# A new work order, an earlier Exp table and ten idle products in a state-space plus gated-MLP kernel

## The chip, the cores and the metric

The kernel runs on one core of a Trainium2 chip. The time is that of one execution on the device, in microseconds (us). The core has five engines that run side by side, each with its own queue of instructions: TensorE (PE in the profile; PEld is its weight load), VectorE (DVE), ScalarE (ACT), GpSimd (POOL) and SyncE (SP), which here only issues DMA transfers. An engine takes its instructions strictly in the order in which the program lists them: one that waits holds up all behind it.

## The reference: what is computed

The input `u` is 2048 tokens of 512 channels. It is normalised, and two branches work on the result; their sum and `u` are the output.

```python
xn = _layernorm(x, axis=-1)
# A: a long convolution along the tokens, its kernel built from 128 complex modes a channel
P = jnp.exp(logdA[:, :, None] * l[None, None, :])
K = jnp.einsum("dn,dnl,dn->dl", Cc, P, dB).real
y = irfft(rfft(xn) * rfft(K)) [:L] + xn * Dskip
# B: a gated MLP with 1792 hidden channels
h = sigmoid(xn @ w_gate) * (xn @ w_up);  out_B = h @ w_down
return x + y + out_B
```

(The two middle lines are shortened.) Inputs and output are bf16.

## The kernel before, in words

**What the work is.** The tokens are 16 tiles of 128. `layernorm` takes their statistics: for tiles 0 to 3 with `bn_stats` on DVE (`stat`, L443 and L445) or, for tiles 1 and 3, in another way on ACT (`stat_act`, L449 to L451). `rstd0` (L457 to L470) makes the reciprocal deviations of tiles 0 to 3 on DVE. `rstd` does it for tiles 4 to 7 on POOL, and for tiles 8 to 15 on POOL too (L479 to L510). Then each tile is normalised (`norm` on DVE, L514, or `norm2` on ACT, L519) and transposed: groups 0 and 1 on TensorE (L524), groups 2 and 3 by DMA (L547).

`params` turns the mode parameters into powers: the time step is `exp(log_dt)` on ACT (L596), a diagonal of it is made on DVE (`dg`, L597, needs the identity), and TensorE multiplies the raw parameters by it (L608, L613). ACT takes four exponentials (L621) and one plain eviction (L624); DVE makes phases (L632 to L637), ACT sines (L640, L641, L646), and DVE and ACT products of them (L654 to L730). An ACT function of another table needs a table load; two tiny activations (L594) make ACT load the Exp and the Sin table at a chosen place.

`glu` is branch B in four groups of 512 tokens: products with gate and up weights (L781), sigmoid on ACT (L807), product on DVE (L814 or L819), down projection (L785), evictions, and adding DMA writes to the output issued by POOL (L840).

Branch A goes by eight chunks of 64 channels: `tables` builds powers of the modes on DVE with squares on ACT (L1244 to L1246, L888 to L892); `kgen`, or for the last two chunks `kgen_late`, multiplies them on TensorE (L976) and transforms them (L946, L999, L1005). `spectrum_x1` and `spectrum_x2` transform the tokens (L762, L1078), `freq` multiplies the spectra (L1125, L1145, L1133 or L1136), and `outq` transforms back and writes (L1192, L1206, L1209, L1212, L1227).

**How it is ordered.** Each step is registered with `add(...)`: engine, an estimate of its time, the steps it comes after, a rank, and sometimes `alt`, a second engine that can do it. Two lists at the end of the file go by the numbers that the steps get in this way. `TURN` is the order in which the steps are written into the program, for all engines; each engine's queue is the part of it that is its own. `OTHER` names the steps that run on their `alt` engine. The estimates are for the planner that made the lists; the program itself only reads `TURN` and `OTHER`:

```python
    def order(self):
        for t in (self.tasks[n] for n in OTHER):
            t.eng, t.cost, t.fn = t.alt[:3]
        return [self.tasks[n] for n in TURN]
```

So everything that the change does to the program lies in the two lists and in the two steps that it adds. In the head, steps 0 to 21 are loads: 0 and 1 the first token tiles, 2 the identity, 3 `s1`, 4 `log_dt`, 5 to 10 the raw parameters (8 is the imaginary part of C), 13, 17 and 16 the token groups 1, 3 and 2, the others MLP weights. Step 101 sets two constants on POOL, 102 to 104 are the seed, the Exp table and `exp(log_dt)`, 105 the diagonal, 26 to 29 the statistics of tiles 0 to 3, 30 is `rstd0`, 43 and 60 are the two `rstd` on POOL, 52 to 59 the statistics of tiles 8 to 15, and 61, 62, 71, 72, 81, 82, 91, 92 their norms.

PSUM tiles come from two pools: `ps_m` with four banks, and `ps_gu` with two pairs of banks (tag `gu`), which the MLP's `pg` and `pu`, and late in the kernel `pw` and `ptv`, take in turn.

Of the kernel before, what the change touches and what calls it, by code (L numbers as in the profile page):

```python
# [11 lines left out]
F32 = mybir.dt.float32  # L12
I32 = mybir.dt.int32
ACT = mybir.ActivationFunctionType
# [237 lines left out]
class _Kernel:  # L252
    def __init__(self, ctx, tc, ins, out):
# [22 lines left out]
        for k in range(len(BLOCKS)):  # L276
            self.freq(k)
            self.outq(k)
        with tc.manual_schedule(engines=ENGINES):
            self.p.emit()  # L280
# [152 lines left out]
    def layernorm(self):  # L433
        nc, add, c = self.nc, self.p.add, self.mult
# [92 lines left out]
        for lo, hi in ((0, 1), (1, 2), (2, 4)):  # L527
            st = [add("DVE", 0.69 if lo else 0.87, lambda i=i: stat(i), [self.ld[f"x{i // 4}{i // 2 * 2 if i < 4 else 0}"]],
                      R["LN2"] + i if lo else R["LN"], use=[self.xg[i // 4]], alt=("ACT", 1.5, lambda i=i: stat_act(i), R["LN"]) if i in (1, 3) else None)
                  for i in range(4 * lo, 4 * hi)]  # L530
            slow = lambda lo=lo, hi=hi: rstd(lo, hi, nc.gpsimd)
            r = add("POOL", 20.0, slow, st, R["LN2"] + 10 * lo) if lo == 1 else add(
                "DVE", 4.2 if lo else 3.4, (lambda lo=lo, hi=hi: rstd(lo, hi, nc.vector)) if lo else rstd0, st, R["LN2"] + 10 * lo if lo else R["LN"],
                alt=("POOL", 16.0, slow, R["LN2"] + 10 * lo) if lo else None)
            self.rstd.append(r)
            for i in range(4 * lo, 4 * hi, 2):
# [5 lines left out]
                if g > 1:  # L542
                    self.norm += n
                    for k in range(2):
                        for kt in range(KT):
# [10 lines left out]
                                          use=[pt, xnT[g]]))  # L556
# [675 lines left out]
def _level(nc, l, o, m, tB, rs, step):  # L1232
# [124 lines left out]
```

## Time and profile before

| | |
|---|---|
| time, median of 3 runs (lowest, highest) | 268.34 us (267.07, 268.83) |
| the profiled execution's own time | 268.08 us |
| its span, first to last instruction | 266.3 us |
| mean granted TensorE clock | 0.990 |
| busy: PE, DVE, ACT, POOL | 236.8, 240.3, 227.8, 65.7 us |
| share of the span | 89%, 90%, 86%, 25% |
| chain that ended last, by engine | PE 44%, DVE 21%, ACT 20%, POOL 6%, issue 5% |
| HBM traffic | 24.61 MB read, 15.73 MB written |

The times are device times of whole executions; the profile is of one of them. Busy time counts an engine's instructions and not the waits of its queue. Matmuls are pipelined and their ends are modelled, so a fully busy PE isn't PE at its peak. A timeline row gives start, duration, engine, line, operation, what it writes and reads, and in brackets how long the engine was idle before it and what ended that. `ACTq` and `SPq` rows are the issue of a DMA by that engine's queue.

### The profile page before, as it was taken

The numbers are of one execution on the slowest core, as the hardware profiler recorded it, in microseconds if no ns is written. First come the engines' busy times: TensorE is split into PE (matmuls) and PEld (weight loads), VectorE is DVE, ScalarE is ACT, GpSimd is POOL, SyncE is SP. The second block draws the span as 40 slices with busy tenths as digits, with TensorE's granted clock in tenths as the row PEclk, the third lists the DMA queues.
The fourth block names the chain that finished last, engine by engine and source line by source line (L and its number), as shares of the span: only waits on it lengthen the run. The fifth ranks groups of instructions, "written<-read, shape, count | busy, mean of one in ns | idle before, by whom it ended". The sixth has DMA issues, their size and how long they took to land.

```text
span 266.3 us, 5528 instructions
## 1 busy us (share of the span) xinstructions
PE 236.8 (89%) x2040; PEld 137.4 (52%) x2040; DVE 240.3 (90%) x450; ACT 227.8 (86%) x369; POOL 65.7 (25%) x107
## 2 busy tenths in 40 slices
PE   0556899998799999999999999999998988988992
PEld 0432345443345545545544654665656575567771
DVE  1699999996999999999999999999999999986860
ACT  3989999979987864799897599999999989998851
POOL 4007977884300003100000210000001020207451
PEclk9999999999999999999999999999999999979998
DMA  7729977101692114589424579888798997979898
GB/s 223 265 81 295 337 232 223 39 2 15 166 258 76 54 40 56 101 183 190 131 87 152 115 166 209 233 216 224 193 272 185 290 218 200 245 152 174 172 95 99
DMA packets 75467, 44.38 MB, mean 167 GB/s; under 512 B 40064, under 2 KB 72064, under 8 KB 74928
## 3 DMA queue, kind: packets, MB, share of 16 engines
q1 hardware_dynamic: 66000, 39.66, 54.7%
q0 software_dynamic: 6752, 3.31, 11.8%
q10 hardware_dynamic: 2688, 1.05, 1.6%
q8 instruction: 16, 0.26, 0.4%
q14 instruction: 11, 0.09, 0.1%
HBM read 24.61 MB, written 15.73 MB: 151 GB/s over the span
## 4 chain that ended last, share of the span: by engine, by line
PE 44%; DVE 21%; ACT 20%; POOL 6%; issue 5%; DMA 1%; ACTq 0%; DVEq 0%; POOLq 0%
PE pg L781 11%; PE pu L781 10%; PE po L785 5%; DVE tB L1244 4%; PE pk L976 4%; DVE G L1245 3%; ACT M L361 2%; PE pv L1136 2%; DVE G L1246 2%; DVE H L1245 2%; ACT hT L807 2%; PE pz L762 2%; PE py L1209 2%; PE pv L1133 2%; PE pkf L1125 2%
## 5 line engine op out<-in xcount | busy, mean ns | idle before, releaser
L781 PEld LDWEIGHTS <-W 128*128 128x128 bf16 x448 | 43.2, 98 | 55.5 <-issue 8.2
L781 PE MATMUL pg<-xnT,W 128*128 128x512 bf16 x224 | 52.9, 379 | 4.0 <-ACT hT L807 3.3
L781 PE MATMUL pu<-xnT,W 128*128 128x512 bf16 x224 | 52.9, 379 | 1.7 <-DVE db L658 1.4
L840 POOL DMA_DIRECT2D out_dram<-gs x16 | 13.7, 874 | 156.9 <-ACT gs L361 94.7
L785 PE MATMUL po<-wd,hT 128*128 128x512 bf16 x224 | 51.2, 379 | 0.0
L785 PEld LDWEIGHTS <-hT 128*128 128x128 bf16 x224 | 21.4, 98 | 22.8 <-issue 0.2
L888 ACT ACTIVATE tB<-G 128x1024 bf16<-128x1024 bf16 (+2 forms) x25 | 30.4, 1214 | 3.1 <-DVE G L892 2.5
L807 ACT ACTIVATE hT<-pg 128x1024 bf16<-128x1024 f32 x28 | 29.3, 1045 | 1.8 <-DVE hT L814 0.8
L361 ACT ACTIVATE hT<-pu 128x1024 bf16<-128x1024 f32 x24 | 24.9, 1039 | 1.3 <-PE pu L781 1.2
L1246 DVE TENSOR_TENSOR G<-G,tB 128x512 bf16<-128x512 bf16 (+2 forms) x35 | 22.3, 641 | 0.3
L1245 DVE TENSOR_TENSOR G<-G,M 128x512 bf16<-128x512 bf16 (+2 forms) x50 | 20.5, 451 | 0.1
L976 PEld LDWEIGHTS <-G 128*128 128x128 bf16 x512 | 17.4, 98 | 4.4 <-DVE G L1246 1.0
L976 PE MATMUL pk<-H,G 128*128 128x64 bf16 x512 | 18.4, 193 | 1.1 <-ACT B L361 0.7
L361 ACT ACTIVATE zs<-pz 128x512 bf16<-128x512 f32 x30 | 17.3, 609 | 2.3 <-PE pz L762 2.3
L1145 DVE TENSOR_TENSOR M<-XX,M 128x1024 bf16<-128x1024 bf16 x28 | 18.9, 684 | 0.3 <-ACT M L361 0.3
L1244 DVE TENSOR_TENSOR tB<-G,M 128x512 bf16<-128x512 bf16 (+2 forms) x27 | 18.9, 705 | 0.2
L1246 DVE TENSOR_TENSOR H<-H,tB 128x512 bf16<-128x512 bf16 (+2 forms) x24 | 18.6, 775 | 0.2
L361 ACT ACTIVATE M<-pkf 128x512 bf16<-128x512 f32 x26 | 16.7, 659 | 0.9 <-PE pkf L1125 0.9
L361 ACT ACTIVATE ksb<-pk 128x512 bf16<-128x512 f32 x28 | 16.5, 627 | 0.9 <-PE pk L978 0.7
L814 DVE TENSOR_TENSOR hT<-hT 128x1024 bf16<-128x1024 bf16 x24 | 16.4, 684 | 0.6 <-ACT hT L361 0.5
L361 ACT ACTIVATE Z<-pzk 128x512 bf16<-128x512 f32 x23 | 13.7, 616 | 2.6 <-PE pzk L946 2.6
L1133 PE MATMUL pv<-M,w 128*128 128x256 bf16 (+1 forms) x128 | 14.6, 251 | 1.1 <-DVE M L1145 1.1
(206 smaller groups left out, 477.3 us busy)
## 6 DMA issues: line engine op xcount, KB each, us to landing
z_scr<-zs SPq DMA_DIRECT2D x32, 128.0 KB, 1.8
XX<-XX SPq DMA_DIRECT2D x28, 128.0 KB, 4.1
zk_scr<-Z SPq DMA_DIRECT2D x3, 1024.0 KB, 7.0
B<-zk_scr SPq DMA_DIRECT2D x12, 256.0 KB, 4.4
B<-z_scr SPq DMA_DIRECT2D x8, 256.0 KB, 3.4
wd<-in_B_w_down_dram SPq DMA_DIRECT2D x1, 1792.0 KB, 13.0
xg<-in_A_u_dram SPq DMA_DIRECT2D x3, 512.0 KB, 5.7
W<-in_B_w_up_dram SPq DMA_DIRECT2D x3, 512.0 KB, 7.0
```

What stands on the lines that cost most here:

```text
L361: return self.p.add("ACT", cost, lambda: nc.scalar.activation(out=dst(), in_=src(), func=ACT.Identity), alt=alt and ("DVE", alt[0], lambda ...
L781: nc.tensor.matmul(p[:, kk, :], w(kt, kk), xnT[:, kt, :], start=(kt == 0), stop=(kt == KT - 1))
L785: nc.tensor.matmul(po[:], hT[:, k, jj * 128:(jj + 1) * 128], wd[:, k, :], start=(k == 0), stop=False)
L807: e1 = add("ACT", 1.03, lambda hT=hT, k=k, pg=pg: nc.scalar.activation(out=hT[:, k:k + 2, :], in_=pg[:], func=ACT.Sigmoid), [m1] + held.ge ...
L814: prods.append(add("DVE", 0.69, lambda hT=hT, u=u, k=k: nc.vector.tensor_tensor(out=hT[:, k:k + 2, :], in0=hT[:, u:u + 2, :], in1=hT[:, k: ...
L888: a = add("ACT", 0.22 + 4 * h * k / 1200.0, lambda: nc.scalar.activation(out=sv(), in_=G[:, :, rs, src, :], func=ACT.Square, scale=float(2 ...
L976: nc.tensor.matmul(pk[:, r], G[:, comp, 8 * q + r].rearrange("p a h -> p (a h)"), H[:, comp, 8 * q + r].rearrange("p b h -> p (b h)"), sta ...
L1133: nc.tensor.matmul(pv[:, n, :], w, pp[:, i, n, :], start=(i == 0), stop=(i == 1))
L1145: d = add("DVE", 0.69, lambda pp=pp, XX=XX, k1=k1, bs=bs: nc.vector.tensor_tensor(out=pp[:], in0=XX[:, :, bs, dx], in1=k1[:].to_broadcast( ...
L1244: lambda: [tt(out=tv()[:, c], in0=l[:, c], in1=mul[1][:, c], op=ALU.mult) for c in cs],
L1245: lambda: [tt(out=inner(o[:, c]), in0=inner(l[:, c]), in1=both(c), op=ALU.mult) for c in ones],
L1246: lambda: [tt(out=o[:, c], in0=o[:, c], in1=tv()[:, flip(c)], op=ALU.add) for c in cs],
```

## The change

The estimates in `layernorm` change, which alters nothing in the program by itself. `TURN` and `OTHER` are replaced as a whole: 1281 steps stand in a new order, and 78 of them change their engine: 75 between ACT and DVE, three output writes between ACT's and SP's queue. Two steps are added, 1281 and 1282: six and four products of the constant identity and `s1`, 256 columns each, into a `ps_gu` pair that nothing reads.

```diff
         for k in range(len(BLOCKS)):
             self.freq(k)
             self.outq(k)
+        for n in (6, 4):
+            pf = self.buf("ps_gu", [128, 2, 512], F32, "pf", 2, "gu")
+            self.p.add("PE", 0.11 * n, lambda pf=pf, n=n: [self.nc.tensor.matmul(
+                pf[:, k % 2, 0:256], self.ident[:], self.s1[:].rearrange("p j f -> p (j f)"), start=True, stop=True)
+                for k in range(n)], [self.w_end, self.ld["ident"], self.ld["s1"]], 1e5, take=[pf])
...
-                      R["LN2"] + i if lo else R["LN"], use=[self.xg[i // 4]], alt=("ACT", 1.5, lambda i=i: stat_act(i), R["LN"]) if i in (1, 3) else None)
+                      R["LN2"] + i if lo else R["LN"], use=[self.xg[i // 4]], alt=("ACT", 1.75, lambda i=i: stat_act(i), R["LN"]) if i in (1, 3) else None)
...
-            r = add("POOL", 20.0, slow, st, R["LN2"] + 10 * lo) if lo == 1 else add(
-                "DVE", 4.2 if lo else 3.4, (lambda lo=lo, hi=hi: rstd(lo, hi, nc.vector)) if lo else rstd0, st, R["LN2"] + 10 * lo if lo else R["LN"],
-                alt=("POOL", 16.0, slow, R["LN2"] + 10 * lo) if lo else None)
+            r = add("POOL", 19.2, slow, st, R["LN2"] + 10 * lo) if lo == 1 else add(
+                "DVE", 4.2 if lo else 3.35, (lambda lo=lo, hi=hi: rstd(lo, hi, nc.vector)) if lo else rstd0, st, R["LN2"] + 10 * lo if lo else R["LN"],
+                alt=("POOL", 20.0, slow, R["LN2"] + 10 * lo) if lo else None)
...
 TURN = (
-    0, 4, 102, 101, 1, 5, 6, 7, 10, 2, 8, 9, 103, 22, 13, 3, 17, 16, 26, 104, 27, 105, 29, 28, 106, 112, 107, 30,
-    114, 111, 115, 113, 110, 121, 11, 108, 117, 116, 36, 31, 184, 23, 32, 109, 185, 118, 187, 33, 188, 175, 120, 172,
...
+    0, 4, 102, 2, 1, 5, 6, 3, 7, 10, 9, 103, 104, 27, 26, 22, 101, 105, 8, 29, 28, 106, 111, 107, 112, 113, 114, 115,
+    110, 13, 17, 30, 121, 11, 108, 109, 117, 116, 36, 31, 184, 32, 187, 185, 118, 175, 33, 176, 172, 119, 34, 177,
+    186, 188, 120, 12, 173, 189, 35, 122, 15, 41, 37, 16, 42, 14, 166, 39, 174, 123, 40, 18, 38, 43, 181, 20, 124,
...
+    1172, 1007, 823, 857, 1119, 1162, 1008, 1009, 868, 860, 1173, 827, 859, 824, 1163, 861, 1281, 829, 1168, 828,
+    838, 1010, 1282, 1178, 830, 1011, 825, 1183, 1179, 862, 1169, 1164, 840, 826, 1174, 1012, 1184, 1130, 1175, 864,
...
 OTHER = (
-    27, 29, 38, 44, 60, 61, 62, 71, 72, 82, 91, 92, 143, 144, 145, 148, 149, 155, 158, 160, 161, 227, 239, 301, 316,
-    372, 411, 422, 487, 565, 584, 594, 624, 632, 739, 765, 778, 788, 830, 844, 873, 876, 878, 884, 888, 901, 908,
-    943, 969, 1032, 1044, 1099, 1195, 1203, 1219, 1221, 1230, 1236, 1247, 1252, 1264, 1266, 1267, 1270, 1272, 1274,
-    1276, 1280)
+    29, 38, 49, 60, 61, 71, 72, 81, 91, 92, 144, 146, 148, 155, 158, 160, 161, 224, 257, 306, 361, 371, 416, 497,
+    565, 571, 573, 616, 618, 642, 664, 668, 739, 761, 767, 778, 788, 844, 881, 884, 892, 899, 936, 943, 992, 1044,
+    1063, 1123, 1191, 1195, 1199, 1209, 1211, 1224, 1230, 1232, 1238, 1245, 1250, 1252, 1260, 1266, 1270, 1276, 1277,
+    1279)
```

In the list's terms: 103 and 104 (Exp table, `exp(log_dt)`) come before 8, ACT's fifth load; 2 (identity) is POOL's first step, before 101; 27 (statistics of tile 1) goes from ACT to DVE; 16 (the load of token group 2) comes after 15 on SP; the norms 61, 71 and so on stand later in ACT's queue, behind other evictions; 1281 stands between 827 and 829, and 1282 between 829 and 1178, on TensorE.

111 rows, old and new, of the table TURN are left out of this document.

## The prediction

> **What bounds the kernel now.** I read the time by windows first, because a mean over the span hides where an engine is short.
>
> ```profile
> 20.00:40.00 20.00, 16.51 (x78) 7.26 (x76) 19.59 (x24) 19.80 (x24) 16.07 (x33) 1.00 0.94 288
> 40.00:60.00 20.00, 20.00 (x109) 9.61 (x107) 19.39 (x40) 18.30 (x25) 16.50 (x33) 1.00 0.27 87
> 60.00:80.00 20.00, 17.26 (x81) 7.75 (x80) 17.35 (x39) 18.29 (x26) 5.02 (x7) 1.00 0.61 148
> 80.00:100.00 20.00, 20.00 (x159) 10.59 (x158) 19.59 (x34) 15.44 (x22) 0.00 (x0) 1.00 0.21 55
> ...
> 160.00:180.00 20.00, 19.67 (x175) 12.02 (x173) 19.93 (x35) 19.40 (x31) 0.00 (x0) 1.00 0.89 220
> ...
> 200.00:220.00 20.00, 18.26 (x252) 13.17 (x249) 19.90 (x41) 18.81 (x36) 2.54 (x3) 1.00 0.95 232
> ```
>
> Columns: window, its length, busy us of PE, PEld, DVE, ACT, POOL, granted clock, DMA share, GB/s. From 20 to 240 us DVE is idle 6.7 us in all, and 2.65 of them lie between 60 and 80. So DVE carries the middle, with PE and ACT close behind: a later start or a hole there reaches the end, and DVE work added there costs its length. DVE's large idle times are the first 13 us and the last 26, where the TensorE work behind the last tables runs. Next I read the timeline of the head, then that around 60 us.
>
> ```profile
> 4.10 0.39 ACTq L354 DMA_DIRECT2D rawn<-in_A_C_im_dram  x1
> ...
> 4.52 1.28 ACT L594 ACT_TABLE_LOAD   x1 [4.52 <-DMA ldt<-in_A_log_dt_dram]
> ...
> 6.43 0.69 DVE L597 TENSOR_TENSOR dg<-ident,dtb 128x512 bf16<-128x512 bf16 x1 [1.58 <-DMA ident<-c_ident]
> ...
> 9.67 0.17 DVE L458 CAST v_b<-mv 128x4 bf16<-128x4 f32 x1 [0.91 <-ACT junk L451]
> ```
>
> ACT's fifth load is issued only at 4.10, when its first (ldt) has landed at 4.08; the Exp table comes after it. DVE waits for the identity, then (L458) for ACT's second set of row statistics.
>
> ```profile
> 60.34 1.52 ACT L519 ACTIVATE xg<-xg,nb,rinv 128x512 bf16<-128x512 bf16 x2 [2.04 <-POOL nb L510]
> ...
> 65.43 0.29 DVE L362 CAST gl<-po 128x128 bf16<-128x128 f32 x1 [1.94 <-ACT gs L361]
> ...
> 69.15 1.02 PE L781 MATMUL pg<-xnT,W 128*128 128x512 bf16 x4 [1.85 <-ACT hT L807]
> ```
>
> ACT's order has a norm of a late token tile next, whose statistics POOL is still computing (41.30 to 60.30); ACT stands 2.04 us, then DVE 1.94 and 0.57, then PE 0.90 and 1.85.
>
> **The head: 2.0 us earlier.** The engines' instructions stand in list order, so the new list can be laid on the old durations. ACT's fourth load ends at 2.67; the table load (1.28) then ends at 3.98, dtb, with ldt landed at 4.08, at about 4.4 in place of 6.11. The fifth load goes out at 4.4 instead of 4.10 and lands at about 9.2 (4.8 us, as before); its transposes end 0.3 us later, but their eviction stands behind the Sin table, which now ends at 11.5, so that costs nothing. Without that cover it would cost 0.3. The identity is issued on POOL at 0.72 instead of 1.71, ahead of two memsets of 0.5 us each that nobody needs before 18 us, and lands 4.6 us later at 5.3. One of ACT's two sets of statistics (1.7 us each) becomes a third on DVE (0.9). DVE: x landed at 3.91, two statistics to 5.76, the diagonal 0.69 to 6.45, the third to 7.36, then the chain L457 to L470, 3.4 us without its waits, to 10.8 in place of 12.83: **2.0 us**. ACT: one set of statistics from 5.06 to 6.8, first Exp behind the first products at 7.6 instead of 9.54: also 2.0. TensorE starts at 6.5 instead of 7.18. From 17 to 58 us no engine but PE has a gap over 0.4 us, and PE's (28 us and before) hang on DVE and ACT; so I let the 2.0 pass whole.
>
> On SP the load of token tiles 8 to 11 moves from 5.45 us to behind the second large weight load (19.88 before, some 17.0 now). Its neighbours there landed 4.1, 5.1 and 6.0 us after issue, in steps of 1.5 us, so it lands at about 22.5. DVE now wants tile 8 right after the products at L654 to L659, at 23.4. It fits by 0.9 us.
>
> **The hole at 60 us: 2.5 us.** POOL's second chain starts when DVE has the last late statistics, 41.22 before. The head's 2.0, and 0.8 us of copies and norms that the new list puts behind them or on ACT, bring that to 38.4; at the 19.0 us that it took the chain ends at 57.5. ACT gets 3.4 us and loses 1.6 there, and its norms come after four copies, three po evictions and a table copy; by the sum of what stands before it the first norm is reached at about 60. The wait is gone with 2.5 us to spare, and with it DVE's 1.94 and 0.57. Next late is DVE's own: its tables start behind L726 to L730, at 58.5, and need parameter copies that ACT now does last, by 58.1. A tie, so I bound this step: 0 (ACT 2.5 us later than I add up) to 2.5, and take 2.5, as both sums come from the same rows.
>
> **Work moved onto DVE: minus 1.4 us.** Evictions and copies change engine throughout. To DVE: 25 of 128x512 at 0.69, 3 norms at 0.40, 3 output evictions at 0.42, the statistics 0.71, 7 small ones at about 0.3. From DVE: 22 at 0.68, 2 norms and 3 copies at 0.41, 2 at 0.55, 7 at about 0.3. Net about 2.2 us, of which 0.7 is the statistics already counted. The other 1.5, less the tenth by which neighbouring DVE rows overlap (one by one they add up to 266 us, its busy time is 240), costs 1.4, as DVE has no slack to hide it. ACT gets 0.6 lighter. Those evictions feed SP's writes and TensorE's next bank; the SP requests between 60 and 145 (transposes, spectrum writes) change places, but their last readers are 5 to 12 us away.
>
> **The tail and the ten products: 0.**
>
> ```profile
> 234.00:235.00 1.00, 0.38 (x8) 0.08 (x3) 1.00 (x3) 1.00 (x3) 0.00 (x0) 1.00 1.18 273
> 235.00:236.00 1.00, 0.96 (x34) 0.99 (x35) 1.00 (x4) 1.00 (x4) 0.00 (x0) 1.00 1.23 269
> 236.00:237.00 1.00, 0.56 (x15) 0.36 (x12) 1.00 (x3) 1.00 (x3) 0.00 (x0) 1.00 1.26 232
> 237.00:238.00 1.00, 1.00 (x10) 1.00 (x11) 0.66 (x3) 1.00 (x2) 0.00 (x0) 0.50 0.24 52
> ...
> 239.00:240.00 1.00, 1.00 (x6) 0.44 (x5) 0.27 (x1) 0.58 (x2) 0.00 (x0) 0.50 0.00 0
> ```
>
> After 3.4 us with thin TensorE work the clock is halved from 237.00 to 240.41, while TensorE is what others wait for. Eight products then took 1.06 instead of 0.61, two 1.06 instead of 0.59: over the 3.4 us some 1.2 us are lost. The ten products stand among the shifting products (L1005) just before; with 256 columns four took 0.60 (L1212), so ten take at most 1.5 us. They use the pair that the first two blocks of the late tables left, whose evictions the L1005 products ahead of them need as well, so they add no wait. Behind them on TensorE stand L1005, L1125 and L1133 products, and the evictions wait for those. TensorE is idle 1.5 us between 231 and 237 (0.24, 0.19, 0.62, 0.04 and 0.44 in its windows): cost between 0 and 1.5, and I take 0, by that idle time. The list also puts 1.2 us of older products (an L1133 and an L1209 set) between the two halves of the last tables' L976 products. With the clock kept that is what the dip took, 4.9 us from half to half as before: 0. If the new products bring nothing, it is 1.2 more.
>
> The Trainium skill (TensorE: Matmul & The Clock Gate, Part 1: The HAM clock gate) says that the half clock follows an idle window of about 3.4 us. By that rule the ten products could change nothing, for in the 3.4 us before 237.00 TensorE was busy 2.3 us and its longest gap was 0.66; the trace, which halves the clock all the same, disagrees. By the rule the sum would be 1.2 us more.
>
> **Sum**: 2.0 + 2.5 − 1.4 = 3.1 us off. The profiled execution took 268.08 us (span 266.3 and 1.8 around it), 0.26 below the median of 268.34; the last 4.7 us after the last eviction at 261.56 (output landing, drains) stay. So **265.0 us**. This kernel's runs lie 267.07 to 268.83 apart, so about 1% (2.7 us) is what can be told from no change.
>
> **Rivals.**
> *The middle eats the gain.* New neighbours on three full engines make new small holes: the tie at 58 us lost by 1.5, and DVE holes elsewhere. For it: the margins that I can add up are 0.4 us (58 us) and 0.9 (tile 8). Against: the old list left DVE 0.6 us of holes from 140 to 230. At 1.5 to 2.5 us: 266.5 to 267.5.
> *The products do nothing*: the half clock falls in the same place or in the TensorE-bound stretch after 240. 1.2 us: 266.2.
> *The dtb path was not the head's bound.* If the loads set it (raw5 landing 8.88), only the diagonal's 0.7 is won of the 2.0: 266.3.
> *Slower: the late token load.* If the load moved on SP is served with the weights behind it instead of before them, as its old neighbours that landed at 28.5 and 30.1 did, or waits for the spectrum writes ahead of it on SP, DVE's queue stands at tile 8 with everything behind it. It decides from a landing after 26.5 us, where the 3.1 is used up; at 30 us the stall is 6.6 us: 268.08 − 3.1 + 6.6 = 271.6.
>
> **How the numbers follow.** Forecast (263.4 to 265.6) 0.50; middle eats it 0.22; products idle 0.07; head 0.05; late load or a hole like it 0.16, of which 0.13 above +1%. The low end: DVE waits nowhere, the statistics' 1.4 is hidden: 263.4, and 0.6 for the runs' scatter: 262.8. The high end takes in the middle rival and the first part of the late-load case: 269.3. Faster by over 1% 0.51, within 1% 0.36, slower 0.13.
>
> **What would show it.** Table load near 2.7 and the first row of L597 near 5.8; L470 at 10.6; no wait of ACT L519 on POOL and none of DVE near 60; DVE busy time up by 2 us; granted clock 1.00 from 20 us to the end of the products; L443 without a wait on xg after 20 us. I am wrong if DVE's idle time between 20 and 240 is above 6 us, or if a DMA stands among DVE's or TensorE's releasers there.

## The result and the profile after

The changed kernel took **265.06 us** (median of four runs, 264.61 to 265.46), the kernel before 267.70 (four, 267.07 to 268.83): ratio 0.9896, 95% interval 0.985 to 0.9942. Timed again unaltered for the experiments, it took 265.09 us over twelve runs beside 267.41 of the kernel before, ratio 0.9921 (0.9893 to 0.9949). The gain is about 1%. Ratios and their intervals are estimated from fast runs alone and are not the quotients of the medians, which are over all runs (three of the experiments' runs were slow). The forecast was 265.0 us; most of this section and of the experiments is about how much of its working deserves that.

The profiled execution took 264.61 us, with a span of 262.8 us (before: 268.08 and 266.3). Line numbers are those before plus five. The page's first part gives the totals:

```profile
PE 237.8 (90%) x2050; PEld 137.5 (52%) x2050; DVE 242.9 (92%) x454; ACT 225.3 (86%) x362; POOL 66.7 (25%) x107
```

DVE works 2.6 us more than before (240.3) and ACT 2.5 us less (227.8), in a span 3.5 us shorter. The windows of the changed kernel, with the columns that the prediction explains:

```profile
0.00:20.00 20.00, 9.07 (x49) 6.21 (x50) 15.18 (x45) 15.49 (x26) 4.11 (x17) 0.91 0.64 188
20.00:40.00 20.00, 19.15 (x81) 8.13 (x80) 19.25 (x23) 19.19 (x24) 15.02 (x29) 0.92 0.89 285
...
60.00:80.00 20.00, 18.54 (x90) 8.36 (x89) 19.74 (x39) 18.85 (x25) 4.74 (x6) 1.00 0.56 121
...
100.00:120.00 20.00, 18.93 (x135) 9.47 (x132) 18.04 (x34) 14.68 (x24) 2.63 (x3) 1.00 0.34 69
...
220.00:240.00 20.00, 18.24 (x262) 13.17 (x262) 19.38 (x42) 19.91 (x40) 3.92 (x5) 1.00 0.80 190
```

Between 60 and 80 us DVE is idle 0.26 us where it was idle 2.65. A new hole of almost 2 us has opened between 100 and 120. The clock column is 1.00 in the tail, but 0.91 and 0.92 in the first two windows: the record shows half speed from 16.5 to 23.3 us.

The head in the changed kernel's timeline (start, duration, engine, line, operation, in brackets the idle time before it and what ended it):

```profile
2.68 1.28 ACT L599 ACT_TABLE_LOAD   x1 [2.68 <-issue]
...
4.16 0.42 ACTq L359 DMA_DIRECT2D rawn<-in_A_C_im_dram  x1
...
5.75 0.69 DVE L602 TENSOR_TENSOR dg<-ident,dtb 128x512 bf16<-128x512 bf16 x1
...
6.50 1.86 PE L613 MATMUL ptd<-dg,rawn 128*128 128x128 bf16 x8 [6.50 <-DVE dg L602]
...
7.45 0.16 DVE L463 CAST v_b<-mv 128x4 bf16<-128x4 f32 x1
...
10.43 0.18 DVE L475 RECIPROCAL rinv<-q 128x4 f32<-128x4 f32 x1
```

The table is loaded while the time step is still on its way, the diagonal starts at 5.75 us instead of 6.43, and DVE's two waits for the identity and for ACT's statistics are gone. The places further on where an engine still stands, from the same timeline:

```profile
23.71 0.70 DVE L448 BATCH_NORM_STATS2 stats<-xg 128x6 f32<-128x512 bf16 x1 [0.65 <-DMA xg<-in_A_u_dram]
...
59.84 0.81 ACT L524 ACTIVATE xg<-xg,nb,rinv 128x512 bf16<-128x512 bf16 x1 [0.56 <-POOL nb L515]
...
65.48 1.89 PE L786 MATMUL pg<-xnT,W 128*128 128x512 bf16 x8 [1.46 <-ACT hT L812]
...
111.58 0.29 DVE L895 TENSOR_TENSOR G<-tB 128x256 bf16<-128x256 bf16 x1 [1.60 <-ACT tB L893]
```

The first row is the token load that the new list moved: DVE waits 0.65 us for it. In the second ACT still waits for POOL, but 0.56 us and no longer 2.04, and DVE does not wait near it. The last row is the new hole: DVE waits for a square on ACT.

### The profile page after: what moved, and what is told of

Read it like the earlier page. It is cut to its first block, busy times and chain, and to the rows that moved or that the text cites. A ratio compares the mean times of both kernels' runs of the same rounds, so it can differ in the third digit from the quotient of the medians.

```text
span 262.8 us, 5553 instructions
## 1 busy us (share of the span) xinstructions
PE 237.8 (90%) x2050; PEld 137.5 (52%) x2050; DVE 242.9 (92%) x454; ACT 225.3 (86%) x362; POOL 66.7 (25%) x107
## 4 chain that ended last, share of the span: by engine, by line
PE 41%; DVE 23%; ACT 15%; DMA 9%; POOL 7%; issue 3%; SPq 1%; DVEq 0%; ACTq 0%; POOLq 0%
PE pg L786 9%; PE pu L786 7%; PE po L790 6%; DMA xg<-in_A_u_dram 4%; PE pk L981 3%; DVE tB L1249 3%; DMA B<-zk_scr 3%; PE pv L1138 3%; DVE stats L448 2%; ACT M L366 2%; PE pkf L1130 2%; PE pv L1141 2%; DVE hT L819 2%; ACT W L366 2%; DMA vp<-v_scr 2%
## 5 line engine op out<-in xcount | busy, mean ns | idle before, releaser
L786 PEld LDWEIGHTS <-W 128*128 128x128 bf16 x448 | 43.8, 99 | 54.1 <-issue 7.7
L786 PE MATMUL pg<-xnT,W 128*128 128x512 bf16 x224 | 54.6, 388 | 3.6 <-ACT hT L812 2.2
L790 PEld LDWEIGHTS <-hT 128*128 128x128 bf16 x224 | 21.3, 98 | 23.4 <-issue 0.6
L366 ACT ACTIVATE M<-pkf 128x512 bf16<-128x512 f32 x28 | 18.5, 673 | 2.7 <-PE pkf L1130 2.6
L1232 POOL DMA_DIRECT2D out_dram<-M x8 | 11.1, 1480 | 25.2 <-ACT M L366 12.3
L366 ACT ACTIVATE ksb<-pk 128x512 bf16<-128x512 f32 x25 | 15.3, 644 | 0.5 <-PE pk L983 0.5
L1250 DVE TENSOR_TENSOR H<-H,M 128x1024 bf16<-128x1024 bf16 (+1 forms) x16 | 15.2, 952 | 0.1
```

The source lines that it names most:

```text
L366: return self.p.add("ACT", cost, lambda: nc.scalar.activation(out=dst(), in_=src(), func=ACT.Identity), alt=alt and ("DVE", alt[0], lambda ...
L786: nc.tensor.matmul(p[:, kk, :], w(kt, kk), xnT[:, kt, :], start=(kt == 0), stop=(kt == KT - 1))
L790: nc.tensor.matmul(po[:], hT[:, k, jj * 128:(jj + 1) * 128], wd[:, k, :], start=(k == 0), stop=False)
L1250: lambda: [tt(out=inner(o[:, c]), in0=inner(l[:, c]), in1=both(c), op=ALU.mult) for c in ones],
```

## The experiments

Each kernel was timed beside runs of the kernel before; ratios are to those. There were three groups, told apart by the median of the kernel before beside them (267.75, 267.41 or 267.88 us); across groups the ratios, with their intervals, compare better than the medians. Only the two lists are edited, except where the diff shows code; a list is cut to the steps concerned.

### One part alone: the head

```diff
 TURN, from the kernel before
-    0, 4, 102, 101, 1, 5, 6, 7, 10, 2, 8, 9, 103, 22, 13, 3, 17, 16, 26, 104, 27, 105,
+    0, 4, 102, 2, 101, 1, 5, 6, 7, 10, 103, 104, 8, 9, 22, 13, 3, 17, 16, 26, 27, 105,
 OTHER: 27 (statistics of tile 1) taken out, so that it runs on DVE
```

> The kernel before with the new head alone: the dt load and the Exp table load ahead of the fifth load on ScalarE's queue, the identity's two GpSimd instructions first on theirs, the statistics of one tile on VectorE. Theory 1 (the lead of 2.0 us runs through to the end): first Exp of the rr chain near 7.6 us (before 9.5), 265.5 to 265.9 us, ratio 0.992 to 0.993. Theory 2 (the middle eats it, since GpSimd's second chain still begins when the old queue lets it, 41.3 us, and ScalarE still waits for it near 60 us): a lead of 2 us at 24 us that is under 0.7 us at 62 us, and 267.0 to 267.7 us, ratio 0.997 to 1.000.

Measured: 266.48 us over twelve runs beside 267.75, ratio 0.994 (0.9916 to 0.9965), so 1.3 to 1.6 us. Neither theory holds as it stood. In the trace the lead is 2.33 us, and it goes through the region of 60 us untouched; ACT waits for POOL as long as before, only earlier:

```profile
58.01 1.52 ACT L519 ACTIVATE xg<-xg,nb,rinv 128x512 bf16<-128x512 bf16 x2 [2.07 <-POOL nb L510]
...
63.10 0.29 DVE L362 CAST gl<-po 128x128 bf16<-128x128 f32 x1 [1.94 <-ACT gs L361]
```

(Before: 60.34 and 65.43, with 2.04 and 1.94.) POOL's chain starts when DVE has the late statistics, so it moved with the head. In this trace the lead shrinks later: at 160 us it is still 2.07, at 200 us 0.83. In between TensorE waits for a transfer for which it stood less than 0.15 us before, and ACT and DVE wait behind it:

```profile
169.99 0.39 PE L1125 MATMUL pkf<-B,w 128*128 128x256 bf16 x2 [0.78 <-DMA B<-zk_scr]
170.42 0.60 ACT L361 ACTIVATE M<-pkf 128x512 bf16<-128x512 f32 x1 [0.88 <-PE pkf L1125]
```

That read went out at 164.16 us and landed at 169.95, after 5.79 us; before it went out at 166.18 and landed at 171.08, after 4.90. Issued 2.0 us earlier, it came only 1.1 us earlier. That the earlier start is the reason isn't shown, and one trace speaks against it. The kernel before with the ten products added (its experiment is below) runs the same steps in the same order up to 234 us. Its execution issued this read 0.6 us later than the kernel before, and the read took 5.88 us:

```profile
166.77 0.58 SPq L359 DMA_DIRECT2D B<-zk_scr  x1
...
172.69 0.39 PE L1130 MATMUL pkf<-B,w 128*128 128x256 bf16 x2 [0.86 <-DMA B<-zk_scr]
```

Between 160 and 200 us that execution falls 1.0 us behind the profiled one of the kernel before, with no lead to lose. Two executions of the changed kernel differ there too: TensorE waits 0.37 us for this read in one and 1.05 in the other. So a lead read from two single traces is uncertain by about 1 us behind 160 us, and how much of the head's lead reaches the end is told by the times: 1.3 to 1.6 us.

### One part alone: the hole at 60 us

```diff
 TURN, from the kernel before
-    154, 307, 71, 308, 165, 315, 62, 306, 82, 24, 299, 92, 312, 142, 300, 81, 72, 485, 495, 317,
-    494, 497, 318, 487, 496, 311, 259,
+    154, 307, 306, 308, 165, 315, 312, 24, 299, 142, 300, 317, 311, 71, 62, 82, 92, 81, 72, 485, 495,
+    494, 497, 318, 487, 496, 259,
```

> The kernel before with one edit: ScalarE's four normalisations of tiles of the second GpSimd chain (tasks 71, 62, 82, 92) stand behind the five evictions and gates that followed them, so that the wait for GpSimd near 60 us has other work ahead of it. Theory 1 (the 2.5 us hole of VectorE at 60 us was on the path that sets the end): the hole shrinks to under 0.7 us, and the time falls by 1.5 to 2.5 us: 265.2 to 266.2 us, ratio 0.991 to 0.995. Theory 2 (slack further on takes it up): the hole is smaller, the end moves by under 0.5 us, ratio 0.998 to 1.000. Theory 3: the wait moves with the instructions and is as long as before, ratio 1.000.

Measured: 266.48 us over nine runs beside 267.75, ratio 0.995 (0.9917 to 0.9983). The order is enough to remove the wait: ACT evicts first, and waits 0.16 us for POOL where it waited 2.04.

```profile
59.87 3.63 ACT L519 ACTIVATE xg<-xg,nb,rinv 128x512 bf16<-128x512 bf16 x5 [0.16 <-POOL nb L510]
...
64.57 0.29 DVE L890 TENSOR_TENSOR G<-tB 128x256 bf16<-128x256 bf16 x1 [1.03 <-ACT tB L888]
```

The hole of 2.5 us on DVE shrinks to 1.03. In the trace DVE's lead goes from 0.48 us ahead of it to 2.05 behind it, a gain of 1.57, and is 1.14 at 237 us: again the loss falls at the read near 170 us, for which TensorE waits 0.57 us here. By the time theory 1 holds in kind, short of its sizes.

### Both parts together

> The kernel before with the new head and with the four normalisations moved behind their followers, both edits together. Alone, each gave 1.27 us. Theory 1 (they add: two separate stalls on the same path): 265.2 us, ratio 0.989 to 0.992, so that these two edits are as fast as the whole change, and the rest of the new order brings nothing. Theory 2 (both come to an end at the same later wait): the gain stays at 1.0 to 1.6 us, ratio 0.994 to 0.996, and the rest of the change is worth another 1.2 us.

Measured: **263.51 us** over five runs (263.06 to 263.75) beside 267.41, ratio **0.9843** (0.9819 to 0.9868). The two add up, and to more than the sum of their medians; the pair is 1.6 us *faster* than the whole change, which took 265.09 us in the same group. Up to 100 us the leads in the traces add (2.33 and 1.57 alone, 3.97 together). Between 160 and 200 us the traces of the single kernels lose 1.24 and 0.91 us and that of the pair only 0.6; as single executions differ by as much there, why two gains of 1.3 make 3.9 is not settled by them.

```profile
57.95 3.63 ACT L519 ACTIVATE xg<-xg,nb,rinv 128x512 bf16<-128x512 bf16 x5 [0.17 <-POOL nb L510]
...
62.66 0.29 DVE L890 TENSOR_TENSOR G<-tB 128x256 bf16<-128x256 bf16 x1 [1.02 <-ACT tB L888]
```

So the question turns round: what does the rest of the new order cost?

### The ten products

On the kernel before, with nothing else changed:

```diff
+        for n in (6, 4):
+            pf = self.buf("ps_gu", [128, 2, 512], F32, "pf", 2, "gu")
...
 TURN, from the kernel before: 1281 after 829, 1282 after 827
```

> The kernel before with the ten unread products alone (six after the first half, four after the second half of the same tile near 235 us, as the changed kernel has them). Theory 1: the half-speed window at 237.0 to 240.4 us is gone, and with it 0.8 to 1.2 us: 266.5 to 266.9 us, ratio 0.995 to 0.997. Theory 2 (VectorE and ScalarE set the pace there, TensorE had slack): the window is gone, the time stays within 0.3 us of 267.7 us. Theory 3 (the products do not hold the clock): the window is still there, time 267.7 to 268.0 us.

Measured: 267.78 us over twelve runs beside 267.75, ratio 0.9996 (0.9974 to 1.0018). The half-speed window is absent from its profile, and the time is the same, as theory 2 has it. The changed kernel without the products:

```diff
-        for n in (6, 4):
-            pf = self.buf("ps_gu", [128, 2, 512], F32, "pf", 2, "gu")
...
 TURN, from the changed kernel: 1281 and 1282 taken out
```

> The changed kernel without its ten unread products, nothing else altered. Theory 1 (the products hold the clock up): the granted clock shows one or two half-speed windows of 3.4 us between 225 and 245 us, as the kernel before has at 237.0 to 240.4, and the time is 0.8 to 1.5 us above the changed kernel's 265.06 us: 265.9 to 266.6 us, ratio to the kernel before 0.993 to 0.996. Theory 2 (the new order alone leaves no stretch of TensorE empty enough): clock 1.00 from 24 us to the end, time as the changed kernel, 264.8 to 265.3 us, or 0.2 us below it, as the ten products no longer stand between the two halves of the work near 235 us; ratio 0.989 to 0.990.

Measured: 265.53 us over eight runs beside 267.75, ratio 0.9916 (0.9888 to 0.9944). The unaltered changed kernel, timed as often:

> The changed kernel once more, unaltered, timed as often as the others so that it can be set beside them. Theory 1 (the ten products are worth nothing, as they were on the kernel before): as the changed kernel without them, 265.3 to 265.7 us, ratio 0.991 to 0.992. Theory 2 (they are worth about 1 us here): 264.6 to 265.1 us, ratio 0.988 to 0.990.

Measured: 265.09 us over twelve, ratio 0.9921 (0.9893 to 0.9949). The median fits theory 2, the ratio theory 1. With and without the products the ratios differ by 0.0005, the medians (of two groups) by 0.4 us: no effect that these runs could show. Theory 1 for the kernel without them is right that a half-speed window appears; the time stays below its range.

The windows of three kernels show where the clock fell and where not. TensorE's busy time is the first pair after the length, the granted clock the third number from the end. The kernel before, around its half-speed window:

```profile
233.59:237.00 3.41, 2.31 (x53) 1.55 (x51) 3.41 (x9) 3.41 (x7) 0.00 (x0) 1.00 1.20 253
237.00:240.41 3.41, 3.41 (x35) 2.85 (x36) 1.93 (x5) 2.66 (x5) 0.00 (x0) 0.50 0.18 40
```

The head alone, which has the old tail, step for step, and no products:

```profile
232.20:235.60 3.40, 2.38 (x50) 1.71 (x50) 3.40 (x9) 3.40 (x8) 0.29 (x1) 1.00 1.14 238
235.60:239.00 3.40, 3.17 (x68) 2.68 (x69) 2.94 (x7) 3.40 (x8) 0.00 (x0) 1.00 0.31 62
```

The changed kernel without products:

```profile
225.80:229.20 3.40, 2.07 (x28) 1.37 (x24) 3.40 (x10) 3.40 (x8) 0.40 (x1) 1.00 0.85 185
229.20:232.60 3.40, 3.29 (x27) 2.57 (x27) 3.40 (x7) 2.90 (x7) 0.00 (x0) 0.50 0.44 100
```

The recorded stretches are multiples of 3.41 us in length, and their edges fall elsewhere in each execution (18.5 us and then 237.00 in the first of these, 20.6 in the second, 10.8 and 229.2 in the third). The old tail lost its clock in the execution that was profiled before, and kept it, without any product, in those of the head, the hole, and both. So the old list has the window at 237 us in some executions and not in others. What it cost there can be read from one row, the sum behind the last tables' square, to the end of the span. Kernel before, span 266.3:

```profile
237.91 0.43 DVE L890 TENSOR_TENSOR G<-tB 128x512 bf16<-128x512 bf16 x1 [0.34 <-ACT tB L888]
```

Head alone, span 264.0:

```profile
237.08 0.43 DVE L890 TENSOR_TENSOR G<-tB 128x512 bf16<-128x512 bf16 x1 [0.35 <-ACT tB L888]
```

Products alone, span 266.7 (its lines, too, are five further on):

```profile
239.62 0.43 DVE L895 TENSOR_TENSOR G<-tB 128x512 bf16<-128x512 bf16 x1 [0.35 <-ACT tB L893]
```

28.4 us against 26.9 and 27.1: 1.3 to 1.5 us, about as predicted. How often it is paid the runs only hint at. Of the 72 runs of the kernel before that stood beside the experiments, eleven have a mean granted clock of 0.987 to 0.992, as the profiled one has (0.990); their median is 269.1 us (266.8 to 269.8), that of the other 61 is 267.7. That most of the eleven lost the clock in the same place would fit, but unprofiled runs don't record the place.

One rival stays open: that the products do keep the clock, and that this is worth little. Of the fourteen profiles of this case eight are of kernels with the products, and none of them has a half-speed window between 25 and 259 us; of the six without, two have one. In the changed kernel the ten products run from 227.6 to 229.4 us. Without them TensorE was busy 2.07 us in the window 225.80 to 229.20 and then lost its clock, and DVE, which keeps its distance to the changed kernel's two executions from 220 to 235 us, loses 0.5 us to both by 237. Six profiles without the products are too few to tell this from chance.

### Mending the waits of the new order

The token load early again, on SP:

```diff
 TURN, from the changed kernel
-    110, 13, 17, 30, 121, 11,
+    110, 13, 17, 16, 30, 121, 11,
```

> The changed kernel with the load of x for tiles 8 to 11 (task 16) issued early on SP again, near 5.8 us, as the kernel before has it. Theory 1 (VectorE's wait of 0.65 us at 23.7 us for this load is on the path): no wait for it, 0.4 to 0.7 us off, ratio 0.987 to 0.989. Theory 2 (the loads that now come behind it are later by its 2 us, and something at the head waits for them): a new wait at 9 to 17 us and a time 0 to 1.0 us above the changed kernel's. Theory 3 (the wait has slack behind it): within 0.3 us.

Measured: 264.61 us over seven runs beside 267.41, ratio 0.990 (0.9864 to 0.9936): 0.5 us by the medians, inside the intervals. DVE's wait at 24 us (1.07 in the unaltered kernel's second profile, 0.65 in the first) is gone. Theory 1 fits the medians, and is not shown.

The square ahead of everything:

```diff
 TURN, from the changed kernel
-    592, 594, 376, 230, 591, 575, 593, 206, 596, 598, 199, 595,
+    592, 594, 598, 376, 230, 591, 575, 593, 206, 596, 199, 595,
```

> The changed kernel with one square of ScalarE (task 598, whose input is ready at 108.66 us and which starts at 110.89) put ahead of the gate and the four evictions that stand before it. Theory 1 (the 1.60 us in which VectorE stands still at 111.6 us are a cost of the new order that reaches the end): that hole under 0.4 us, and 0.8 to 1.6 us off: 263.6 to 264.5 us, ratio 0.984 to 0.988. Theory 2 (TensorE, which then waits 0.66 us longer for the gate and the evictions, or a later wait, sets the end): time within 0.4 us of the changed kernel's.

Measured: 265.02 us over eleven runs, ratio 0.9926 (0.9898 to 0.9954), as the unaltered kernel. The edit was a poor one. It puts the square ahead of 593, which writes the entries that the square reads; so the square takes them unfinished, which changes values and not the amount of work, and 593 waits until it has read: DVE stood 1.09 us for it at 109.48, and 0.46 at 112.77. Once more, with the square behind 593 (that order, rather than the scratch buffer of which the expectation speaks, is what matters):

```diff
 TURN, from the changed kernel
-    592, 594, 376, 230, 591, 575, 593, 206, 596, 598, 199, 595,
+    592, 594, 591, 593, 596, 598, 376, 230, 575, 206, 199, 595,
```

> The changed kernel with the same square (task 598) moved again, and this time behind the two DVE instructions that it shares a scratch buffer with (591, 593), so that the order in which buffers are handed out is kept; ahead of it no longer stand the gate 376 and the evictions 230, 575, 206. Theory 1 (the 1.60 us hole of VectorE at 111.6 us sets the end): hole under 0.3 us, 0.8 to 1.6 us off: 263.5 to 264.3 us, ratio 0.985 to 0.989. Theory 2 (TensorE waits longer for the gate and the evictions and hands the loss on, as it did when the square stood ahead of all): within 0.3 us of the changed kernel's 265.1 us, ratio 0.991 to 0.993.

Measured: 265.07 us over ten runs beside 267.88, ratio 0.9882 (0.9858 to 0.9906). The median is that of the unaltered kernel, 265.09, to 0.02, as theory 2 has it; the ratio is lower by 0.004 and would fit theory 1. The kernel before was slower beside this one (267.88 against 267.41), which is part of that, so the times alone don't decide. In its trace the hole is not gone but one step on:

```profile
109.78 0.28 DVE L895 TENSOR_TENSOR G<-tB 128x256 bf16<-128x256 bf16 x1
...
112.44 0.69 DVE L819 TENSOR_TENSOR hT<-hT 128x1024 bf16<-128x1024 bf16 x1 [1.50 <-ACT hT L366]
```

And ACT's rows of the same stretch:

```profile
106.91 0.63 ACT L366 ACTIVATE H<-B 128x512 bf16<-128x512 bf16 x1 [2.88 <-PE pk L983]
...
108.50 0.63 ACT L893 ACTIVATE tB<-G 128x512 bf16<-128x512 bf16 x1
109.03 1.00 ACT L812 ACTIVATE hT<-pg 128x1024 bf16<-128x1024 f32 x1
...
111.36 1.05 ACT L366 ACTIVATE hT<-pu 128x1024 bf16<-128x1024 f32 x1
```

From 106.91 on ACT works without a pause, and whatever is taken forward there pushes the next thing back; DVE's next step now waits for the eviction of 111.36. ACT is behind because it stood 2.88 us in front of a copy into the table `H`, which has two buffers in turn, until TensorE had read the one that it takes. By 140 us DVE is no further ahead than in the changed kernel. So the trace speaks for theory 2, with ACT as the engine that hands the loss on. (That copy, step 632, is on DVE in the kernel before; putting it back was not tried.) Both mends in one:

> The changed kernel with both mends: the load of x for tiles 8 to 11 early again, and the square moved as in the run beside this one. Theory 1 (these two waits of VectorE, 0.65 to 1.1 us at 24 us and 1.60 us at 111.6 us, are what the new order loses against the kernel before with its two edits, 263.51 us): 263.0 to 263.7 us, ratio 0.982 to 0.986. Theory 2 (the loss lies elsewhere, in the work moved or spread in many small waits): 264.4 to 264.8 us, ratio 0.988 to 0.990.

Measured: 264.79 us over six runs beside 267.88, ratio 0.9875 (0.9838 to 0.9913). The median is theory 2's, and the ratio lies between the two theories' ranges. Beside it in the same group stands the pair with one norm more (last experiment), 264.11 us and 0.985: the two intervals overlap, so whether mending these two waits brings the new order to the pair's level is not settled. The median says that it doesn't.

The evictions behind 235 us shared out as before:

```diff
 OTHER, from the changed kernel
-    881, 892, 1123, 1191, 1199, 1209, 1211, 1224, 1232, 1238, 1245, 1250, 1260, 1279
+    876, 878, 888, 1203, 1219, 1221, 1236, 1247, 1264, 1272, 1274
```

> The changed kernel with the evictions after 235 us shared out between VectorE and ScalarE as in the kernel before (14 back to ScalarE, 11 to VectorE), order unchanged. Theory 1 (the tail is set by TensorE and by the waits from one stage to the next, so VectorE's extra 1.5 us of work there costs nothing): VectorE busy 1.2 to 2.0 us less, the time within 0.4 us of the changed kernel's or above it. Theory 2 (what was predicted: work moved onto VectorE is paid in full): 0.8 to 1.5 us off, ratio 0.985 to 0.989.

Measured: 266.12 us over twelve runs beside 267.88, ratio 0.9929 (0.9902 to 0.9957). By the medians that is 1.0 us above the changed kernel, by the ratios (0.9921, in another group) 0.2 us: not faster, and perhaps slower. DVE is busy 241.3 us instead of 242.9, and waits instead:

```profile
241.47 0.69 DVE L367 CAST Z<-pw 128x512 bf16<-128x512 f32 x1 [1.94 <-ACT Z L366]
```

Theory 1 holds: in the tail DVE's extra 1.6 us cost nothing. Whether they save time, because DVE waits for ACT in this row, is not shown.

### One more mend of the faster version

```diff
 TURN, from the kernel with head and hole edits: 72 (a norm of a late tile) from before 485 to behind 501
```

> The kernel before with head and hole edits, and one normalisation more (task 72, whose reader runs 20 us later) behind the copy and the square that VectorE waits for at 62.7 us. Theory 1 (VectorE's 1.02 us wait there is on the path): the wait falls to 0.2 to 0.5 us and 0.5 to 0.8 us come off: 262.7 to 263.1 us, ratio 0.981 to 0.983. Theory 2 (TensorE, which works without a pause from 62 us on, takes it up): 263.3 to 263.7 us, ratio 0.984 to 0.986.

Measured: 264.11 us over six runs beside 267.88, ratio 0.985 (0.9813 to 0.9887), the same as without it. Theory 2, but with another engine than it names. DVE was 0.63 us ahead just behind the mended place and 0.09 at 75 us; in place of 1.02 us at 62.66 it waits 0.32, 0.10, 0.26 and 0.28 at 62.0, 66.6, 67.6 and 81.0, each time for ACT:

```profile
62.00:66.00 4.00, 3.53 (x17) 1.56 (x16) 3.91 (x12) 4.00 (x7) 1.41 (x3) 1.00 0.17 25
66.00:70.00 4.00, 4.00 (x21) 1.77 (x19) 3.60 (x8) 4.00 (x5) 0.88 (x2) 1.00 0.86 264
```

ACT is busy 4.00 of 4.00 us in both windows: its sum of work, not its order, sets DVE's pace there.

## Why the prediction was right, and where its working was not

**The number.** 265.0 us was forecast, 265.06 measured. The agreement rests partly on two errors that cancel. The sum started from a profiled execution of 268.08 us and a median of 268.34 over three runs; over the 72 later runs the kernel before is at 267.77. And 3.1 us were taken off, while the changed kernel gains 2.3 to 2.6 by the medians of the two comparisons: 3.9 by the two edits, where 4.5 was forecast, less 1.6 by the rest of the order, where 1.4 was. The spans give 3.5 us, but 1.3 to 1.5 of that is the half-speed window that the profiled execution of before happened to have.

**The head, 2.0 us.** Right in mechanism, and somewhat more in size: the mean-and-deviation chain of the first tiles ends 2.2 us earlier, and the head alone leads by 2.33. Two details were off and covered: the identity went out at 1.23 us, not 0.72, and landed at 5.66 instead of 5.3, and the diagonal still started at 5.75, because DVE had the second statistics until 5.68. "I let the 2.0 pass whole" is the step that is not borne out: by the times the head alone is worth 1.3 to 1.6 us. Its trace loses 1.24 between 160 and 200 us, where TensorE waits for a read; but that read is late without any lead, too, so the cause is open.

**The token load.** Predicted to land at 22.5 us and to be wanted at 23.4; it landed at 23.69, and DVE waited 0.65. The direction of the risk was seen, the landing was put 1.2 us too early. The slower rival, which starts from a landing after 26.5, did not come.

**The hole at 60 us, 2.5 us.** Its cause was right: the same four norms put behind other evictions in the old list remove ACT's wait. By these norms alone DVE gains 1.57, and waits 1.03 for ACT's other work; the changed kernel leaves DVE idle 0.26 us of the stretch instead of 2.65, and which of its other moves does the rest was not tried. In the changed kernel POOL's second chain took 21.15 us (38.65 to 59.80), not the 19.0 copied from before, so ACT reached the norm before POOL and the "2.5 us to spare" became a wait of 0.56; DVE had no gap there all the same.

**Work moved onto DVE, minus 1.4.** Right in sum, and not settled in kind. Against the kernel with head and hole edits the changed kernel is 1.6 us slower, and that is what the rest of the new order costs. The traces show where it has arisen: at the sum behind the last tables' square.

Head and hole edits, span 261.7, then the changed kernel, span 262.8:

```profile
234.84 0.43 DVE L890 TENSOR_TENSOR G<-tB 128x512 bf16<-128x512 bf16 x1 [0.35 <-ACT tB L888]
```

```profile
235.98 0.43 DVE L895 TENSOR_TENSOR G<-tB 128x512 bf16<-128x512 bf16 x1
```

From these rows to the end both take 26.8 to 26.9 us, so the loss lies ahead of them. There DVE is busy 1.4 us more in the changed kernel (226.4 us against 225.0) and, from 20 us on, idle 0.4 us less: it has more to do by then, and doesn't wait more. That speaks for work on DVE as the cost, though not for the forecast's reason. Of the 1.8 us by which DVE's whole work differs (242.9 and 241.1), 1.6 belong to the evictions behind 235 us; with those shared out as before it is 241.3, and the kernel is no faster. In that run's trace DVE has 0.7 us less to do ahead of the row and waits 1.2 us more. So "DVE has no slack to hide it" failed for the moves behind 235 us, which hold nearly all of the net work moved. The moves ahead of 235 us nearly cancel in sum; what they and the new order cost was not tried apart, and stays open.

**The tail and the ten products, 0.** "If the new products bring nothing, it is 1.2 more" failed. On the old list and on the new one they bring nothing that the runs can tell from no change, and without them the new list took 265.53 us, not 266.2: the loss that they were to prevent comes in some executions only. The prediction weighed one statement of the Trainium skill (TensorE: Matmul & The Clock Gate, Part 1: The HAM clock gate) and left out another that bears on this. The same section says that the window over which the clock is decided is free-running and does not start with the kernel; the traces agree, with edges at 10.8, 16.5, 20.6 or 237.0 us, in steps of 3.41. The statement that was weighed, that half speed follows an idle window, they contradict again: TensorE was busy 2.31 of 3.41 us and 2.07 of 3.40 before the two drops shown above.

**What would show it.** Table load (2.68), diagonal (5.75), L475 (10.43), DVE's busy time (2.6 up) and DVE's idle time from 20 to 240 us (5.3, bound 6) came as written. A clock of 1.00 from 20 us did not (23.3), nor ACT's norm without a wait for POOL (0.56), nor L448 without a wait: a DMA stands among DVE's releasers (23.71), and one of 1.35 us among TensorE's (212.92; 0.68 before). By its own words the prediction would be wrong by that last sign, though the time agreed; the kernel before shows the same sign for TensorE, so it couldn't tell much. Of the rivals, "the middle eats the gain" is the one that is half true: an order with that head (the token load left early) and that mended hole, and nothing else, is 1.6 us faster.

## What to carry to other kernels

Take a gain apart before believing it: the two edits that matter here, in the old order, beat the whole replanned list by 1.6 us, 263.51 against 265.09. Don't build a term on something that one profiled execution shows once, such as a clock window or a late read; see whether the same stretch shows it in another execution first. And before a wait of the busiest engine is mended, look whether the engine that it waits for has any idle time left in that stretch: where it had none, as ACT here at 62 to 70 and at 107 to 113 us, the wait only moved.

## What the hardware showed that was not expected

- **The clock before its first record.** In the profile of before the record begins at 18.5 us with full speed. The products ahead of it ran at half speed: transposes (L524, 128 columns) start 107 ns apart at 16 us and 56 ns apart at 20 us. In the other kernels the last change to full speed in the head lies between 13.3 and 25.0 us. The kernel with the hole edit alone has the old head; it ran at half speed from 14.8 to 25.0 us, and its DVE is still 0.48 us ahead of the kernel before at 61 us. So half speed from 18.5 to 25 us cost nothing that shows in this pair of traces.
- **A read whose time varies from execution to execution.** The 256 KB read for which TensorE waits near 170 us took 4.90 us in the kernel before, 5.79 with the head alone, 5.54 with the hole edit alone, 5.56 with both and 5.88 with the products alone, issued at 166.18, 164.16, 164.12, 162.46 and 166.77 us. The quickest and the slowest of the five are those of the two kernels that run the same steps up to there, so the time of issue doesn't explain it. In two executions of the changed kernel it took 4.29 and 4.97 us. What else it met there was not separated.
